# A newly searched order for the work ahead of the MLP, on five engines

## The chip, the cores and the metric

The kernel runs on one core of a Trainium2 chip. The core has five engines with an instruction queue each: TensorE (PE: matrix products and transposes, out of PSUM only by other engines), VectorE (DVE), ScalarE (ACT), GpSimd (POOL), and SyncE (SP), which here only issues DMAs; ScalarE issues some too. The metric is the time of one execution on the device in microseconds, as the median of several runs, together with one profiled execution of the kernel.

## The reference

Two layers follow each other on x of 2048 rows by 576. The first is a linear attention with 32 heads of 18 features; its feature map is a pair of softmaxes. The second is an MLP of width 4608 behind two layer norms.

```python
def _A_ref(x, wqkv, w_phi, wo):
    q, k, v = ...                                  # x @ wqkv, 32 heads of 18
    pq = jnp.einsum("bhsd,hdf->bhsf", q, w_phi)
    pk = jnp.einsum("bhsd,hdf->bhsf", k, w_phi)
    phi_q = jnp.concatenate([_softmax(pq, axis=-1), _softmax(-pq, axis=-1)], axis=-1)
    phi_k = jnp.concatenate([_softmax(pk, axis=-1), _softmax(-pk, axis=-1)], axis=-1)
    kv = jnp.einsum("bhsf,bhsd->bhfd", phi_k, v)
    z  = jnp.einsum("bhsf->bhf", phi_k)
    num = jnp.einsum("bhqf,bhfd->bhqd", phi_q, kv)
    den = jnp.einsum("bhqf,bhf->bhq", phi_q, z)[..., None] + 1e-6
    o = num / den
    return ... @ wo

def _B_ref(x, w1, b1, w2, b2):
    y = _layernorm(x, axis=-1)
    h = _gelu(jnp.einsum("bsd,df->bsf", y, w1) + b1)
    return jnp.einsum("bsf,fd->bsd", h, w2) + b2

h = x + _A_ref(_layernorm(x, axis=-1), A_wqkv, A_w_phi, A_wo)
h2 = h + _B_ref(_layernorm(h, axis=-1), B_w1, B_b1, B_w2, B_b2)
```

## The kernel before

The rows of x are taken as 16 tiles of 128, in eight pairs p = 0 to 7; a tile of a pair is called a = 0 or 1. Each layer norm is statistics on VectorE (`stats`), a power -1/2 on POOL (`power`, `power1`), and a scaling of the tile on VectorE or ScalarE (`scale`; for ScalarE POOL first works out the shift in `centre`).

The work ahead of the MLP is cut into some 60 kinds of steps, each a small function. Those that matter here:

- `load_wk`, `load_x`, `load_values`, `turn_wq`: the first loads, all issued by SyncE but one. `turn_wq` loads the query part of the weights turned, by transposing DMAs. `load_wk(c)` brings block c of the key part plainly (block 4 in two halves, called 4 and 5); TensorE turns it (`flip_mm`, line 423) into PSUM and `flip_ev` (line 429) copies it out.
- `fold_mm` (line 447) multiplies the turned weights by the block-diagonal feature weights that POOL spreads out in `spread`; `fold_ev` (line 458) casts the product from PSUM to SBUF. After it a projection of x gives the arguments of the softmaxes at once.
- `turn_n_mm` and `turn_n_ev` (line 412) turn the tiles of pairs 0 and 1 on TensorE; from pair 2 on SyncE does it by a transposing DMA (`turn_dma`, line 362).
- `key_n_mm`, `value_n_mm`, `query_n_mm` and their `_tail` (line 511) are the projections of pairs 0 and 1; `key_mm`, `value_mm`, `query_mm` (line 485) those of pairs 2 to 7, in two halves i of 18 matmuls. ScalarE takes the exponentials out of PSUM (`key_n_exp`, `key_exp`, `query_exp`, lines 575 and 548) or casts the values (`value_n_ev`, `value_ev`).
- `key_sum` and `key_n_sum` (lines 610 and 632, with a reciprocal) add up the exponentials of the keys on VectorE, and `key_weigh`, `key_n_weigh` (lines 616 and 641) scale them by it, on POOL or, where the step says `vec`, on VectorE. Each (p, i, a) is one weighing of 128 by 576.
- `sums(p, a)` (line 728) adds keys times values of a tile into `acc_kv`, after its weighings. After all sixteen, `table`, `combine_mm`, `divide`, `turn_o_mm`, `residual_mm` and `second` finish the first pair, `rescale` and `turn2_mm` make its input to the MLP, and the MLP starts (line 1326). Eight query halves are kept back to fill TensorE between these.
- `load_w1(q, n)` brings piece n of six of a quarter q of w1. Quarter 0 lies in the place of the key and query weights, quarter 1 in that of the values and keys. The MLP's first pass over w1 reads quarter 0 first.
- `warm` and `filler` are matmuls on an identity whose results nobody reads.

Three PSUM tiles of two banks (`two0` to `two2`), five tiles of exponentials (`exk`) and eleven larger tiles (`home`) are handed out by queues in the code: a step that takes a slot waits until its earlier user's result has been read.

What sets the order: the calls stand in a list in the source, and each engine executes its instructions in the order of the calls, under a manual schedule. Semaphores make each instruction wait for its data, so an engine stands when the next instruction in its row isn't ready, also if a later one would be. DMAs of SyncE and ScalarE share eight semaphores in turn, so a DMA is issued only after the one eight places ahead of it has landed. The MLP's part stands behind the list and isn't touched.

Of the kernel before, what the change touches and what calls it, by code (L numbers as in the profile page):

```python
# [47 lines left out]
def kernel(  # L48
# [889 lines left out]

    warm(6)
    filler(4)  # L940
    stats(0, 0)
    load_wk(2, syn)
    filler(4)
    filler(4)
    window_masks()
# [3 lines left out]
    filler(4)  # L949
    load_wk(0, syn)  # L950
    flip_mm(0)
    spread(2)
    power1(0, 0, pool)
    stats(0, 1)
    spread(3)
    power1(0, 1, pool)
    flip_ev(0, act)
    scale(0, 0, vec)
    turn_n_mm(0, 0)
    turn_n_ev(0, 0, act)  # L960
    load_x(2, 4, syn)
    stats(1, 0)
    spread(0)
    scale(0, 1, vec)
    load_wk(3, syn)
    load_wk(1, syn)
    flip_mm(3)
    flip_ev(3, dve)
    stats(1, 1)
    spread(1)  # L970
    filler(4)
    flip_mm(1)
    load_x(4, 6, syn)
    stats(2, 0)
    load_wk(4, syn)
    spread(4)
    flip_ev(1, act)
    power(1, pool)
    centre(1, 0)
    fold_mm("k", 2)  # L980
    fold_ev("k", 2, act)
    turn_n_mm(0, 1)
    turn_n_ev(0, 1, act)
    load_wk(5, syn)
    fold_mm("k", 1)
    fold_ev("k", 1, act)
    fold_mm("k", 0)
    flip_mm(4)
    flip_ev(4, dve)
    fold_ev("k", 0, act)  # L990
    fold_mm("k", 3)
    load_values(2, syn)
    fold_mm("k", 4)
    fold_ev("k", 3, act)
    key_n_mm(0, 0)
    stats(2, 1)
    scale(1, 1, vec)
    load_x(8, 12, syn)
    stats(4, 0)
    stats(4, 1)  # L1000
    fold_ev("k", 4, act)
    key_n_tail(0)
    scale(1, 0, act)
    key_n_exp(0, 0)
    filler(4)
    turn_n_mm(1, 0)
    key_n_mm(0, 1)
    stats(5, 0)
    power(2, pool)
    key_n_sum(0, 0)  # L1010
    turn_n_mm(1, 1)
    turn_n_ev(1, 0, act)
    key_n_mm(1, 0)
    turn_n_ev(1, 1, act)
    key_n_tail(1)
    key_n_exp(0, 1)
    key_n_sum(0, 1)
    stats(5, 1)
    key_n_mm(1, 1)
    key_n_exp(1, 0)  # L1020
    key_n_exp(1, 1)
    load_values(0, syn)
    value_n_mm(1, 1)
    turn_wq(0)
    turn_wq(2)
    load_values(1, syn)
    turn_wq(1)
    value_n_tail(1)
    value_n_ev(1, 1, act)
    fold_mm("q", 4)  # L1030
    load_b1()
    load_x(6, 8, syn)
    key_n_weigh(0, 0, 1, pool)
    power(4, pool)
    load_x(12, 16, syn)
    key_n_weigh(0, 1, 0, pool)
    swap_k(1)
    key_n_weigh(0, 1, 1, pool)
    stats(3, 0)
    stats(3, 1)  # L1040
    fold_ev("q", 4, act)
    fold_mm("q", 1)
    fold_ev("q", 1, act)
    value_n_mm(1, 0)
    value_n_ev(1, 0, act)
    scale(2, 1, vec)
    fold_mm("q", 0)
    fold_ev("q", 0, act)
    scale(4, 0, vec)
    centre(2, 0)  # L1050
    scale(2, 0, act)
    key_n_sum(1, 1)
    value_n_mm(0, 1)
    load_values(4, syn)
    swap_q(0)
    value_n_tail(0)
# [24 lines left out]
    key_n_sum(1, 0)
    stats(7, 0)
    key_n_weigh(1, 1, 0, pool)
    key_n_weigh(1, 0, 0, pool)
    key_n_weigh(1, 1, 1, pool)
    turn_dma(2)
    stats(6, 0)
    stats(7, 1)
    power(7, pool)
    scale(5, 0, vec)  # L1090
    stats(6, 1)
    key_n_weigh(1, 0, 1, pool)
    centre(7, 1)
    power(6, pool)
    query_n_exp(1, 1)
    query_n_exp(0, 0)
    scale(3, 0, act)
    query_n_exp(0, 1)
    query_n_sum(0, 1)
    query_weigh(0, 1, 1, pool)  # L1100
    key_mm(2, 0)
    key_exp(2, 0)
    turn_dma(4)
    key_mm(4, 0)
    scale(5, 1, vec)
    key_exp(4, 0)
    query_weigh(0, 0, 1, pool)
    key_sum(4, 0)
    key_weigh(4, 0, 1, pool)
    centre(6, 1)  # L1110
    key_mm(4, 1)
    load_values(3, syn)
    value_mm(2, 0)
    value_ev(2, 0, act)
    key_exp(4, 1)
    key_sum(4, 1)
    key_weigh(4, 1, 1, pool)
    key_weigh(4, 1, 0, pool)
    scale(7, 0, vec)
    key_sum(2, 0)  # L1120
    swap_q(2)
    turn_b1()
    key_mm(2, 1)
    key_weigh(4, 0, 0, pool)
    key_weigh(2, 0, 1, pool)
    value_mm(4, 0)
    key_weigh(2, 0, 0, pool)
    key_exp(2, 1)
    value_ev(4, 0, act)
    load_w1(0, 3, sca)  # L1130
    value_mm(4, 1)
    turn_dma(3)
    key_mm(3, 1)
    value_ev(4, 1, act)
    scale(6, 0, vec)
    key_sum(2, 1)
    key_weigh(2, 1, 1, pool)
    swap_q(1)
    key_weigh(2, 1, 0, pool)
    query_n_sum(0, 0)  # L1140
    query_weigh(0, 1, 0, pool)
    key_exp(3, 1)
    scale(6, 1, act)
    turn_dma(5)
    value_mm(2, 1)
    value_ev(2, 1, act)
    scale(7, 1, act)
    value_mm(3, 1)
    value_mm(5, 0)
    value_ev(5, 0, act)  # L1150
    load_w1(0, 0, syn)
    value_ev(3, 1, act)
    key_mm(5, 1)
    key_exp(5, 1)
    key_mm(3, 0)
    key_exp(3, 0)
    key_sum(5, 1)
    key_weigh(5, 1, 1, pool)
    key_mm(5, 0)
    key_sum(3, 0)  # L1160
    key_weigh(3, 0, 1, pool)
    key_exp(5, 0)
    key_sum(5, 0)
    key_sum(3, 1)
    key_weigh(3, 0, 0, pool)
    key_weigh(5, 1, 0, pool)
    load_w1(0, 5, sca)
    sums(1, 1)
    turn_dma(6)
    turn_dma(7)  # L1170
    sums(4, 0)
    sums(4, 1)
    sums(1, 0)
    query_mm(4, 0)
    query_exp(4, 0)
    load_wo(1, sca)
    load_wo(0, syn)
    load_w1(0, 4, syn)
    load_w1(0, 2, syn)
    value_mm(7, 1)  # L1180
    key_mm(6, 0)
    value_ev(7, 1, act)
    key_exp(6, 0)
    key_weigh(5, 0, 1, pool)
    key_weigh(3, 1, 1, vec)
    query_weigh(0, 0, 0, pool)
    key_weigh(3, 1, 0, pool)
    key_mm(7, 1)
    value_mm(5, 1)
    key_exp(7, 1)  # L1190
    key_sum(7, 1)
    value_ev(5, 1, act)
    key_mm(7, 0)
    key_exp(7, 0)
    key_mm(6, 1)
    key_exp(6, 1)
    value_mm(6, 1)
    value_mm(6, 0)
    value_ev(6, 0, act)
    value_ev(6, 1, act)  # L1200
    value_mm(7, 0)
    turn_q(0)
    value_ev(7, 0, act)
    load_w1(0, 1, sca)
    key_weigh(7, 1, 1, pool)
    key_sum(7, 0)
    key_weigh(7, 0, 0, pool)
    query_mm(6, 0)
    value_mm(3, 0)
    value_ev(3, 0, act)  # L1210
    query_exp(6, 0)
    key_sum(6, 0)
    key_sum(6, 1)
    query_mm(5, 1)
    key_weigh(7, 1, 0, vec)
    query_mm(2, 0)
    sums(3, 1)
    key_weigh(7, 0, 1, pool)
    sums(3, 0)
    key_weigh(5, 0, 0, pool)  # L1220
    sums(2, 1)
    key_weigh(6, 1, 1, vec)
    sums(5, 1)
    sums(7, 0)
    sums(7, 1)
    sums(5, 0)
    sums(2, 0)
    query_exp(5, 1)
    query_exp(2, 0)
    load_b2()  # L1230
    key_weigh(6, 0, 1, pool)
    key_weigh(6, 0, 0, pool)
    sums(6, 1)
# [254 lines left out]
```

## Time and profile before

| | us |
|---|---|
| three runs | 387.64, 387.71, 391.0 |
| median | 387.71 |
| the profiled execution: time | 387.87 |
| the profiled execution: span of the core | 386.1 |
| DMA, HBM read / written | 16.62 MB / 2.36 MB |

The profile's rows begin with the start and the length in us, then the engine, the line of the source, the operation, what it writes and reads, the shapes, and the number of merged instructions; in brackets stands how long the engine was idle before it and what ended that. PEld is the weight load of TensorE, which overlaps its matmuls. SPq and ACTq are the DMA issues of SyncE and ScalarE. A matmul's end is modelled, so busy TensorE can hide short stalls; the starts are measured.

### The profile page before, as it was taken

The page shows a single profiled execution, that of the slowest core. Times are in us where ns is not written, and L with a number is a line of the kernel's source. Part 1 is how long each engine was busy: PE and PEld are TensorE (multiplying, and loading weights), DVE is VectorE, ACT ScalarE, POOL GpSimd, SP SyncE. Part 2 cuts the span into 40 slices and gives each one's busy share as a digit, 9 for nine tenths or more (in the row PEclk, how much of TensorE's full clock was granted, in tenths as well). Part 3 has the DMA queues.
Part 4 walks back from the last instruction along what each step waited for, and adds up shares of the span by engine and source line. Part 5 has one row for each costly group of instructions (what it writes and reads, how often), then busy time and mean ns, then how long its engine had stood idle before and what let it go on. Part 6 is the DMA issues. An engine that isn't in the chain of part 4 may idle for free.

```text
span 386.1 us, 9945 instructions
## 1 busy us (share of the span) xinstructions
PE 380.0 (98%) x4353; PEld 265.4 (69%) x4354; DVE 166.5 (43%) x363; ACT 161.4 (42%) x289; POOL 114.3 (30%) x156
## 2 busy tenths in 40 slices
PE   7999999999999999999999999999999999999997
PEld 5677778789878887744467886444677754447773
DVE  6998997791379387670047330000560100000100
ACT  4999875698204730066630001666200026661000
POOL 6397995042425572054013101000131110000120
PEclk9999999999999999999999999999999999999999
DMA  7999998999536686450007534000071000000000
GB/s 199 270 168 187 203 217 139 256 332 244 139 69 111 108 98 121 86 119 4 0 2 97 78 87 63 2 3 0 2 120 36 17 17 0 2 2 0 17 31 16
DMA packets 72975, 35.35 MB, mean 92 GB/s; under 512 B 59940, under 2 KB 69860, under 8 KB 72804
## 3 DMA queue, kind: packets, MB, share of 16 engines
q1 hardware_dynamic: 70832, 31.23, 40.8%
q10 hardware_dynamic: 2100, 3.49, 3.9%
q8 instruction: 34, 0.56, 0.6%
q14 instruction: 9, 0.07, 0.1%
HBM read 16.62 MB, written 2.36 MB: 49 GB/s over the span
## 4 chain that ended last, share of the span: by engine, by line
PE 94%; ACT 2%; DMA 2%; DVE 1%; issue 0%; SPq 0%
PE acc L1371 37%; PE acc L1326 37%; PE two L485 10%; PE acc L868 4%; PE two L511 3%; PE acc_kv L728 1%; DMA w<-in_A_wqkv_dram 1%; ACT exk L575 1%; DMA xh<-in_A_x_dram 1%; PE acc L818 1%; PE pn L818 1%; PE two L868 1%; PE two L447 1%; DVE ob L832 1%; ACT home L412 0%; ACT shared L458 0%
## 5 line engine op out<-in xcount | busy, mean ns | idle before, releaser
L1348 ACT ACTIVATE home<-acc,b1col 128x512 bf16<-128x512 f32 (+1 forms) x180 | 98.2, 599 | 168.6 <-PE acc L1326 165.8
L1371 PE MATMUL acc<-w,home 128*128 128x288 bf16 (+2 forms) x1151 | 143.2, 286 | 0.1
L1326 PE MATMUL acc<-shared,w 64*128 64x512 bf16 (+2 forms) x1638 | 141.7, 331 | 0.2 <-ACT shared L384 0.2
L1371 PEld LDWEIGHTS <-home 128*128 128x128 bf16 x1152 | 109.4, 98 | 32.1 <-issue 1.8
L1326 PEld LDWEIGHTS <-w 64*128 64x128 bf16 x1638 | 80.4, 94 | 60.3 <-issue 1.4
L1375 DVE TENSOR_TENSOR ot<-acc,hb 128x288 bf16<-128x288 f32 (+2 forms) x32 | 14.4, 452 | 106.4 <-PE acc L1371 96.6
L1360 POOL TENSOR_TENSOR hb<-xh,b2bc 128x576 f32<-128x576 bf16 x16 | 20.4, 1273 | 104.5 <-DVE ot L1375 104.5
L674 POOL TENSOR_TENSOR padded<-home,rq 128x540 bf16<-128x540 bf16 x32 | 34.9, 1104 | 37.7 <-DVE rq L666 14.3
L877 DVE TENSOR_TENSOR xh<-acc,xh 128x288 bf16<-128x288 f32 x28 | 11.4, 447 | 69.9 <-PE acc L868 69.9
L292 POOL TENSOR_TENSOR rs<-va,mhalf 128x1 f32<-128x1 f32 x16 | 8.8, 550 | 108.7 <-DVE va L290 108.4
L485 PEld LDWEIGHTS <-home 64*128 64x128 bf16 x648 | 31.2, 94 | 8.3 <-issue 0.2
L616 POOL TENSOR_TENSOR exk<-exk,rk 128x576 bf16<-128x576 bf16 x20 | 23.6, 1219 | 0.9 <-DVE rk L612 0.9
L548 ACT ACTIVATE home<-two 128x576 bf16<-128x576 f32 x24 | 13.9, 657 | 7.9 <-PE two L485 4.5
L868 PEld LDWEIGHTS <-shared 64*128 64x128 bf16 x288 | 13.9, 94 | 4.3 <-issue 0.5
L296 DVE TENSOR_SCALAR shared<-xh,mv,rs 128x576 bf16<-128x576 bf16 x32 | 16.1, 566 | 0.5 <-DMA shared<-shared 0.5
L868 PE MATMUL acc<-wo,shared 64*128 64x288 bf16 x252 | 16.3, 283 | 0.0
L610 DVE TENSOR_REDUCE sk<-exk 128x64 f32<-128x1152 bf16 x12 | 15.9, 1326 | 0.7 <-ACT exk L548 0.7
L665 DVE TENSOR_REDUCE sk<-home 128x64 f32<-128x1152 bf16 x12 | 15.7, 1310 | 0.0
L831 DVE RECIPROCAL rec<-acc 128x18 f32<-128x18 f32 (+1 forms) x14 | 3.5, 248 | 26.8 <-PE acc L818 26.8
L485 PE MATMUL two<-wqp,home 64*128 64x288 bf16 x216 | 14.4, 283 | 0.0
L485 PE MATMUL two<-wv,home 64*128 64x288 bf16 x216 | 14.4, 283 | 0.0
L548 ACT ACTIVATE exk<-two 128x576 bf16<-128x576 f32 x24 | 13.8, 659 | 1.3 <-PE two L485 1.3
(97 smaller groups left out, 263.3 us busy)
## 6 DMA issues: line engine op xcount, KB each, us to landing
w<-in_B_w_dram SPq DMA_DIRECT2D x18, 432.0 KB, 8.4
w<-in_B_w_dram ACTq DMA_DIRECT2D x6, 432.0 KB, 11.0
out_dram<-ot SPq DMA_DIRECT2D x15, 144.0 KB, 2.2
xh<-in_A_x_dram SPq DMA_DIRECT2D x2, 576.0 KB
xh<-in_A_x_dram SPq DMA_DIRECT2D x3, 288.0 KB, 4.0
wo<-in_A_wo_dram SPq DMA_DIRECT2D x1, 648.0 KB, 6.5
wo<-in_A_wo_dram ACTq DMA_DIRECT2D x1, 648.0 KB, 11.0
w<-in_A_wqkv_dram SPq DMA_DIRECT2D x4, 158.0 KB, 3.1
```

The lines of the kernel that those rows point to most:

```text
L296: nc.vector.tensor_scalar(dst, src, mv[:, i, 0:1], rs[:, i : i + 1], ALU.subtract, ALU.mult)
L485: nc.tensor.matmul(dst[:, a, 0:HALF], lhs[rows, c, :], w[rows, slot, i * HALF : (i + 1) * HALF], start=(n == 0), stop=(n == KC - 1),)
L548: nc.scalar.activation(rows[:, :, i * HH : (i + 1) * HH, s, :], flight[key, p, i][:, :, 0:HALF].rearrange("p a (h f) -> p a h f", f=DH), A ...
L610: nc.vector.tensor_reduce(sk[:, :, :], part_of(dst, i), AX.X, ALU.add)
L616: eng.tensor_tensor(part, part, flight["r" + key, p, i][:, a, :].rearrange("p (h o) -> p h o", o=1).to_broadcast([P, NH, DH]), ALU.mult,)
L665: nc.vector.tensor_reduce(sk[:, :, :], part_of(phiq[p], i), AX.X, ALU.add)
L674: eng.tensor_tensor(padded[:, a, g0 * P : (g0 + 5) * P].rearrange("p (g k) -> p g k", k=P)[:, :, 0:STEP].rearrange("p g (h f) -> p g h f", ...
L868: nc.tensor.matmul(pa[a], oT[p % 2][rows, c, :], wo[rows, c, cs], start=(c == 0), stop=(c == KC - 1),)
L1326: nc.tensor.matmul(ph[half][:, lo:hi], w1[p_ // 9][rows, c, p_ % 9 * P : (p_ % 9 + 1) * P], ln2T[rows, c, base + lo : base + hi], start=(c ...
L1348: nc.scalar.activation(hidden(m), ph[half][:, 0:width], AF.Gelu_apprx_tanh, bias=b1col[:, m : m + 1], scale=1.0,)
L1360: nc.gpsimd.tensor_tensor(hb[:, :], xh[:, t, :], b2bc[:, :], ALU.add)
L1371: nc.tensor.matmul(po[:, :], hidden(m)[:, i_ * P : (i_ + 1) * P], w2[m // 18][:, m % 18, cs], start=(j == 0), stop=(j == NM - 1),)
```

## The change

The list of calls ahead of the MLP is replaced by another with the same steps. The instructions of TensorE fall by eight filler matmuls (and their weight loads). Some steps go to another engine: two casts of folded query weights go from ScalarE to VectorE; three more scalings of x go from VectorE to ScalarE, each with a shift on POOL; one weighing of keys goes from VectorE to POOL, and VectorE's three others are of other tiles; one copy of the turned attention result goes from VectorE to ScalarE. The key weights' halves 4 and 5 are loaded ahead of further rows of x, the transposed query weights ahead of the value weights, and piece 1 of quarter 0 of w1 later. The diff, cut to the places that matter here:

```diff
+    window_masks()
     warm(6)
-    filler(4)
-    stats(0, 0)
     load_wk(2, syn)
-    filler(4)
-    filler(4)
-    window_masks()
     filler(4)
     flip_mm(2)
     flip_ev(2, act)
-    filler(4)
     load_wk(0, syn)
     flip_mm(0)
...
+    turn_wq(2)
     filler(4)
...
+    turn_wq(1)
+    fold_mm("q", 1)
+    fold_mm("q", 3)
...
+    fold_ev("q", 3, dve)
+    fold_ev("q", 1, act)
+    fold_ev("q", 0, act)
...
+    load_values(0, syn)
+    value_n_mm(1, 0)
...
+    fold_ev("q", 4, dve)
...
-    load_w1(0, 1, sca)
...
-    key_weigh(6, 1, 0, vec)
     sums(6, 0)
+    table(0)
+    query_mm(2, 1)
+    combine_mm(1, 0, two)
+    query_exp(2, 1)
     load_w1(1, 0, sca)
...
+    query_mm(7, 1)
+    query_exp(7, 1)
+    load_w1(0, 1, sca)
```

Three places in rows of the built program follow, first the kernel before, then the changed one. Numbers behind a name tell uses of a buffer apart; the figure directly behind `two` is the PSUM slot.

ScalarE behind its first instruction, in the opening: L429 copies a turned weight block, L412 a turned half of x, L458 casts folded key weights.

```order
L429 COPY w1_0_108<-two1_172 128x5x128
L429 COPY w1_0_108<-two2_184 128x5x128
L412 COPY home0_63<-two0_205 128x512
L429 COPY w1_0_108<-two2_184 128x5x128
L458 CAST shared_109<-two0_256 128x576
L412 COPY home0_63<-two1_263 128x640
L458 CAST shared_109<-two2_272 128x576
```

```order
L429 COPY w1_0_108<-two1_155 128x5x128
L429 COPY w1_0_108<-two2_163 128x5x128
L412 COPY home0_63<-two0_190 128x512
L429 COPY w1_0_108<-two1_155 128x5x128
L458 CAST shared_109<-two0_224 128x576
L458 CAST shared_109<-two1_243 128x576
L458 CAST shared_109<-two2_259 128x576
```

The fourth row was the copy of block 1 (slot 2, shared with block 0) and is now that of block 3 (slot 1, shared with block 2); block 1 goes to VectorE, and the second half of x behind the five casts.

SyncE's loads from the second pair of key weight blocks on: L171 are key weights, L192 rows of x, L161 transposed query weights, L179 and L187 value weights.

```order
L171 DMA w1_0_108<-in_A_wqkv_dram 128x632 x2
L192 DMA xh_74<-in_A_x_dram 128x1152
L171 DMA w1_0_108<-in_A_wqkv_dram 64x632 x2
L187 DMA wv_110<-in_A_wqkv_dram 64x576
L192 DMA xh_74<-in_A_x_dram 128x2304
L179 DMA wv_110<-in_A_wqkv_dram 128x4x576
L161 DMA_TRANSPOSE w1_0_108<-in_A_wqkv_dram 128x576
L161 DMA_TRANSPOSE w1_0_108<-in_A_wqkv_dram 128x2x576
L179 DMA wv_110<-in_A_wqkv_dram 128x576
```

```order
L171 DMA w1_0_108<-in_A_wqkv_dram 128x632 x2
L171 DMA w1_0_108<-in_A_wqkv_dram 64x632 x2
L192 DMA xh_74<-in_A_x_dram 128x1152 x2
L192 DMA xh_74<-in_A_x_dram 128x2304
L161 DMA_TRANSPOSE w1_0_108<-in_A_wqkv_dram 128x576
L161 DMA_TRANSPOSE w1_0_108<-in_A_wqkv_dram 128x2x576 x2
L179 DMA wv_110<-in_A_wqkv_dram 128x4x576
L179 DMA wv_110<-in_A_wqkv_dram 128x576
```

The large load of value weights (128x4x576) stood ahead of the transposed loads and stands behind all three.

ScalarE's queue around the last sums: L548 are exponentials, L535 casts of values, L759 DMAs of w1 (into `w1_0` quarter 0, into `w1_1` quarter 1), L384 a copy of the turned attention result.

```order
L535 CAST vals_107<-two2_1275 128x2x16x18
L759 DMA w1_0_108<-in_B_w1_dram 64x3x1152
L535 CAST vals_107<-two1_1323 128x2x16x18
L548 ACTIVATE home7_70<-two0_1304 128x2x16x18 x2
L548 ACTIVATE home8_71<-two2_1353 128x2x16x18 x2
L548 ACTIVATE home9_72<-two1_1373 128x2x16x18 x2
L759 DMA w1_1_1518<-in_B_w1_dram 64x3x1152 x2
```

```order
L548 ACTIVATE home8_71<-two1_1512 128x2x16x18 x2
L759 DMA w1_1_1545<-in_B_w1_dram 64x3x1152
L548 ACTIVATE home10_73<-two2_1572 128x2x16x18 x2
L759 DMA w1_0_108<-in_B_w1_dram 64x3x1152
L548 ACTIVATE home9_72<-two1_1594 128x2x16x18 x2
L384 COPY shared_109<-pT_1621 128x512
L759 DMA w1_1_1545<-in_B_w1_dram 64x3x1152
```

The last piece of quarter 0 stood three exponentials ahead of the first pieces of quarter 1, and now stands behind one of them.

More of the change, by code (lines that the diff above doesn't have):

```diff
@@ L1133 @@
[L1133 to L1155, printed above, removed]
```

526 lines of the change are left out of this document (270 added, 256 removed).

## The prediction

> **What bounds the kernel now.** The busy shares come first, then a table of stages cut at four places: 5.65 us (first real transposes on TensorE), 24.39 (first sums of keys times values), 65.64 (last sums issued) and 80.06 (first MLP matmul).
>
> ```profile
> PE 380.0 (98%) x4353; PEld 265.4 (69%) x4354; DVE 166.5 (43%) x363; ACT 161.4 (42%) x289; POOL 114.3 (30%) x156
> ...
> core 0: us, PE busy (x) PEld busy (x) DVE busy (x) ACT busy (x) POOL busy (x), PEclk, DMA share, GB/s
> 5.65:24.39 18.74, 17.22 (x190) 12.67 (x189) 17.33 (x44) 16.95 (x29) 11.02 (x21) 1.00 0.97 239
> 24.39:65.64 41.25, 41.25 (x724) 32.53 (x721) 38.02 (x52) 33.51 (x58) 36.51 (x41) 1.00 1.04 189
> 65.64:80.06 14.42, 13.95 (x232) 10.94 (x230) 10.80 (x32) 8.84 (x17) 1.12 (x2) 1.00 0.92 229
> 80.06:386.10 306.04, 303.30 (x3195) 206.64 (x3195) 97.63 (x230) 100.63 (x184) 61.82 (x72) 1.00 0.32 61
> ```
>
> TensorE sets the end. A new order can give back only holes on it: none in the third stage (41.25 of 41.25), 18.74 - 17.22 = 1.52 us in the second, 14.42 - 13.95 = 0.47 in the fourth, and what short stalls the modelled ends of matmuls hide. The fifth stage, 306 us, keeps its instructions. So the gain is capped near 2 us plus what fillers cost, while a loss has no cap. The timeline shows the opening, by SyncE, TensorE and ScalarE (start, length, instructions). Behind it stand sizes with median times from issue to landing, and the shortest, median and longest landing of the six loads of key weights (L171).
>
> ```profile
> 1.24 0.89 SPq L171 DMA_DIRECT2D w<-in_A_wqkv_dram  x2
> 7.68 0.42 SPq L179 DMA_DIRECT2D wv<-in_A_wqkv_dram  x1
> 8.15 4.86 SPq L161 DMA_TRANSPOSE w<-in_A_wqkv_dram  x2
> 13.68 1.37 SPq L161 DMA_TRANSPOSE w<-in_A_wqkv_dram  x1
> ...
> 1.41 2.74 PE L285 MATMUL two<-ident 128*128 128x512 bf16 x6 [1.41 <-POOL ones L210]
> 3.94 1.91 PE L276 MATMUL acc_kv<-ident 128*128 128x128 bf16 x16
> 5.65 0.50 PE L423 MATMUL two<-ident,w 128*128 128x128 bf16 x5
> 8.16 0.45 PE L423 MATMUL two<-ident,w 128*128 128x128 bf16 x5 [0.57 <-DMA w<-in_A_wqkv_dram]
> 8.45 0.43 PE L447 MATMUL two<-w 128*128 128x126 bf16 x5
> 21.43 1.50 PE L511 MATMUL two<-wv,home 128*128 128x288 bf16 x12
> 23.14 1.15 PE L511 MATMUL two<-wv,home 128*128 128x288 bf16 x8
> 24.12 0.43 PE L447 MATMUL two<-w 128*128 128x126 bf16 x5
> ...
> 8.65 0.69 ACT L429 COPY w<-two 128x640 bf16<-128x640 bf16 x1 [0.69 <-PE two L423]
> 10.36 2.36 ACT L458 CAST shared<-two 128x576 bf16<-128x576 f32 x4
> 12.60 0.88 ACT L308 ACTIVATE shared<-xh,nb,rs 128x576 bf16<-128x576 bf16 x1
> 13.37 1.19 ACT L575 ACTIVATE exk<-two 128x576 bf16<-128x576 f32 x2
> 15.38 0.69 ACT L412 COPY home<-two 128x640 bf16<-128x640 bf16 x1 [0.34 <-PE two L407]
> 15.97 3.38 ACT L575 ACTIVATE exk<-two 128x576 bf16<-128x576 f32 x6
> ...
> wv<-in_A_wqkv_dram SPq DMA_DIRECT2D x1, 576.0 KB, 6.2
> wv<-in_A_wqkv_dram SPq DMA_DIRECT2D x1, 144.0 KB, 4.2
> home<-shared SPq DMA_TRANSPOSE x6, 3.8
> ...
> DMA to landing us min/median/max: 2.9/3.1/4.3
> ```
>
> From about 6 to 25 us ScalarE is the chain (16.95 of 18.74 busy): it empties PSUM, and TensorE waits for slots. The copy of a weight block at 8.65 (L429) came late because its transposes waited for a load until 8.16.
>
> **The change, part by part.**
>
> *Opening.* Block 2 of the key weights is issued at 1.24 and block 0 ends its issue at 2.13. With the median landing of 3.1 us block 2 is there near 4.8; block 0, third in the queue, at 5.2 to 6.4, and I take 6.1. One filler group now follows the warm-up instead of four, so TensorE stands from 4.37 (four fillers at 107 ns, from 16 of them between 3.94 and 5.65) to 4.8, and again from 5.35 to 6.1. Eight of 28 filler matmuls are gone in all. ScalarE then runs without the 0.69 us hole: block 0 copied from 6.6, the first turned half of x from 7.2, block 3 from 7.75. Casts of folded keys come 0.57 us apart ((2.36 - 0.64) / 3) at 8.3, 8.95, 9.75, 10.3 and 10.85. The third waits because block 1 still arrives at 8.16 and its copy, by VectorE, frees a slot only near 9.1. The second turned half follows at 11.4, the scaling at 12.0 (before 12.60), the first exponentials at 12.75 (before 13.37), the six others at 15.2 to 18.55 (before 15.97 to 19.35): 0.6, then 0.8 us ahead.
>
> *Folded queries and values.* Here most of that lead goes. The query folds need slots that the last exponentials hold until 18.55, so TensorE stands about 0.8 us; two more scalings of x on ScalarE (0.88 each) stand among the evictions, against two casts given to VectorE. From 19.15 TensorE runs without a hole: four value halves of 0.98 (23.14 to 24.12), two tails of 0.35 (1.50 with a tail, 1.15 without) and one fold of about 0.3, to 24.1. The same work ended at 24.39 before: 0.3 gained. But the large load of value weights is moved behind the three transposed loads. Those take SyncE 4.86 + 1.37 = 6.2 us from about 7.6, so it is issued near 14.4 instead of 7.68 and lands 4.2 to 6.2 later, 18.6 to 20.6, where 19.15 is needed. The nearer row is the large one, but it was queued behind much more; I take 19.35, 0.2 lost. Turned halves of x have less room in the third stage: SyncE's transposes of pairs 4 and 6 follow ScalarE's scalings near 26.5 and 42.4, take 3.8, and are needed at about 31.0 and 46.7. That is 0.7 and 0.5 spare, cost 0. Opening and values together: -0.1, with ends at -1.5 (the second stage's holes gone) and +1.2.
>
> *Weighings.* POOL and VectorE scale the keys in time for the last sums. The rows are POOL's first weighing, VectorE's sums, and the weighings of both engines with shortest, median and longest duration.
>
> ```profile
> 17.54 1.16 POOL L641 TENSOR_TENSOR exk<-exk,rk 128x576 bf16<-128x576 bf16 x1 [3.94 <-DVE rk L637]
> ...
> L610 DVE TENSOR_REDUCE sk<-exk x12: 1294/1342/1353, 34.0 to 58.6; 128x64 f32<-128x1152 bf16 x12
> ...
> L616 POOL TENSOR_TENSOR exk<-exk,rk x20: 1159/1168/1686, 36.2 to 61.5; 128x576 bf16<-128x576 bf16 x20
> ...
> L616 DVE TENSOR_TENSOR exk<-exk,rk x4: 744/1244/1716, 52.0 to 63.8; 128x576 bf16<-128x576 bf16 x4
> ...
> 60.50 4.01 DVE L616 TENSOR_TENSOR exk<-exk,rk 128x576 bf16<-128x576 bf16 x3
> 65.75 0.50 DVE L743 TENSOR_TENSOR kvm<-acc_kv,wmask 128x324 bf16<-128x324 f32 x1 [1.24 <-PE acc_kv L728]
> ```
>
> VectorE keeps three weighings of four, POOL gets one more (28 + 1 = 29) and starts at 20.5 instead of 17.54, since the first sum of keys waits for the last exponentials and takes 1.34 and a reciprocal of some 0.5. With 29 x 1.17 = 33.9, and 8 us of other work (the third stage's 36.51 less 24 weighings leaves 8.4), it ends at 62.4; I find one wait of 2.0 for a sum that four statistics stand ahead of on VectorE: 64.4. The last sums need it at 65.1, so 0.7 is spare: cost 0. If every one of VectorE's three runs into POOL's at the 1716 of its slowest instead of 744, it is 2.9 more, and 2.2 late; that is the upper end. Nothing is gained below, since TensorE has no hole there.
>
> The DVE rows show weighings that take 744 alone and (4.01 / 3) 1337 ns beside POOL's. [...]
>
> *Table, division, residual.* The sequence of two covering query blocks between combine and turn is kept, and so is the wait on VectorE's division; one of two copies after it goes to ScalarE, hidden beside the query block behind it. Cost 0, at most +-0.47 (the fourth stage's hole).
>
> *First MLP weights.* One of the six pieces of the first quarter of w1 was issued by ScalarE at 58.09. It now stands behind an exponential of the query, after the first piece of the next quarter.
>
> ```profile
> 58.09 0.62 ACTq L759 DMA_DIRECT2D w<-in_B_w_dram  x1
> 65.87 1.54 ACTq L759 DMA_DIRECT2D w<-in_B_w_dram  x2
> ...
> w<-in_B_w_dram SPq DMA_DIRECT2D x18, 432.0 KB, 8.4
> w<-in_B_w_dram ACTq DMA_DIRECT2D x6, 432.0 KB, 11.0
> ...
> DMA to landing us min/median/max: 4.8/8.6/13.5
> ...
> 80.06 4.18 PE L1326 MATMUL acc<-shared,w 64*128 64x128 bf16 x85 [0.17 <-ACT shared L384]
> ```
>
> Two query blocks and two combines after 65.64 put its issue near 68.9, and the second matmul of the MLP reads it at 79.95. Landing may take 11.05. The rows say 8.6 (all), 11.0 (ScalarE's queue), 13.5 (the slowest): 0 to 2.5 us late. It is second in its queue behind one piece, where the slowest case is presumably the third of three, so I take 10.5: on time, cost 0. SyncE's weights move only among themselves; the rest of MLP weights is needed 10 us later or more.
>
> *Sum.* -0.1 + 0 + 0 + 0 = -0.1 on the profiled 387.87: 387.8. The median of the runs shown, 387.71, stands 0.16 below that execution, so I forecast 387.6. Own range of this case: 386.4 to 388.3.
>
> **Rivals.**
>
> *MLP weights late* (slower): the moved piece of w1 takes 12.1 instead of 10.5, between 11.0 and 13.5, or ScalarE's next load, which waits for an older one, holds back the copy that feeds the MLP. It decides from 11.05 on. For it: the median of that queue is within 0.1 of the limit. Against: only one piece lies ahead of it. Price 1.05: 388.7.
>
> *A late clock* (slower): TensorE issued 128-column matmuls every 107 ns until 5.65, and 5 in 0.29 us at 8.16 (58 ns each). It had then worked since 1.41 without a hole. The new holes at 4.37 and 5.35 may postpone this. [...] No run here yet shows whether a gap of 0.4 counts.
>
> *Values late* (slower): the load lands at 20.6. TensorE has no other work in order there: 1.2 lost, 388.8.
>
> *Weighings late* (slower): POOL ends 1.2 late through overlap with VectorE: 388.8. For it: both engines are busy 36 to 38 of 41 us in that stage. Against: VectorE has three scalings fewer.
>
> *The loads land as before and all holes go* (faster): 1.4 gained, 386.2. Against it: ScalarE's chain stays, and it gains 0.8 at most.
>
> **How the numbers follow.** Forecast 0.42; MLP weights late 0.26; late clock 0.12; values late 0.08; weighings late 0.09; all holes gone 0.03. Nearly all of it lies between 386.4 and 389.4, the slow cases with 0.5 on top; two of them together, or one beyond its bound, are left out with the 386.2. A change of 1% is 3.9 us, about what a measurement of this kernel can tell from none. Faster by that would need more than all holes: 0.02. Slower by that needs three mishaps or a wait not found here: 0.05. Within 1%: 0.93.
>
> **What would show it.** Right: block 3 copied by ScalarE near 7.75, six exponentials ending near 18.6, values done near 24.1, the last sums issued near 65.5, MLP from 79.9 with no DMA named ahead of it. Wrong: 107 ns matmuls after 6.1; a DMA as releaser of the first MLP weights or of value matmuls; TensorE waiting for POOL or VectorE between 60 and 66; a hole in the third stage, where now there is none.

## The result, and the profile after

| | before | after |
|---|---|---|
| median of six runs each | 387.86 us | 393.17 us |
| lowest and highest | 387.64, 391.0 | 392.53, 394.64 |
| ratio, with its 95% interval | | 1.0134 (1.011 to 1.0158) |
| the profiled execution: time, span | 387.87, 386.1 | 394.64, 392.9 |

The changed kernel is slower by 1.3%, where no change was forecast, and the time lies outside the range (386.4 to 388.3). The profiled execution of it is its slowest, 1.5 us above the median. Its stages follow with the same columns. The first border stays at 5.65 us, the others are at the same events as before (values done, last sums issued, first MLP matmul):

```profile
5.65:24.05 18.40, 16.65 (x178) 12.17 (x179) 17.45 (x44) 17.39 (x30) 11.46 (x26) 1.00 1.02 233
24.05:68.10 44.05, 41.83 (x722) 33.44 (x720) 42.31 (x50) 34.31 (x60) 37.16 (x41) 1.00 0.89 170
68.10:82.55 14.45, 14.04 (x233) 10.66 (x230) 10.33 (x30) 8.56 (x15) 1.11 (x2) 1.00 0.95 202
82.55:392.90 310.35, 305.07 (x3198) 207.82 (x3196) 97.76 (x230) 101.57 (x185) 61.87 (x72) 0.99 0.32 63
```

The stages changed by -0.34, +2.80, +0.03 and +4.31 us. The third stage has a hole now (44.05 of span, 41.83 busy). The MLP lost 4.3 us: it stood for 310.35 - 305.07 = 5.28 instead of 2.74, and its same matmuls took 1.77 us more at a granted clock of 0.99.

*Around the last sums*, in the timeline of the changed kernel:

```profile
54.51 7.89 POOL L616 TENSOR_TENSOR exk<-exk,rk 128x576 bf16<-128x576 bf16 x7
...
55.93 7.76 DVE L616 TENSOR_TENSOR exk<-exk,rk 128x576 bf16<-128x576 bf16 x2
...
62.29 3.03 PE L728 MATMUL acc_kv<-vals,exk 128*128 128x57 bf16 x93
...
63.61 1.34 DVE L610 TENSOR_REDUCE sk<-exk 128x64 f32<-128x1152 bf16 x1
65.05 0.55 DVE L612 RECIPROCAL rk<-sk 128x64 f32<-128x64 f32 x1
65.68 1.16 POOL L616 TENSOR_TENSOR exk<-exk,rk 128x576 bf16<-128x576 bf16 x1 [3.28 <-DVE rk L612]
65.71 1.75 DVE L616 TENSOR_TENSOR exk<-exk,rk 128x576 bf16<-128x576 bf16 x1
67.52 0.65 PE L728 MATMUL acc_kv<-vals,exk 128*128 128x57 bf16 x17 [2.20 <-DVE exk L616]
```

VectorE's two weighings of pair 7 took 7.76 us. The first of them took 7.09 and ended 0.62 after POOL's row of weighings (54.51 + 7.89 = 62.40), the second took 0.75. These two are new on VectorE; (6, 1, 1) it had before, too, and (3, 1, 1), its weighing at 52 in the kernel before, is POOL's now. Behind the two stands the last sum of keys on VectorE; POOL waits 3.28 for that, and TensorE 2.20 for the weighing behind it. The same view of the kernel before has one row of sums:

```profile
62.39 3.32 PE L728 MATMUL acc_kv<-vals,exk 128*128 128x57 bf16 x110
```

So the sums begin 0.10 earlier (62.29) and take 68.10 - 62.29 = 5.81 instead of 3.25: +2.56.

*At the MLP's start*, in the same timeline of the changed kernel:

```profile
82.55 0.23 PE L1327 MATMUL acc<-shared,w 64*128 64x128 bf16 x1
...
83.30 0.45 PE L1327 MATMUL acc<-shared,w 64*128 64x128 bf16 x9 [0.53 <-DMA w<-in_B_w_dram]
...
84.48 0.60 ACTq L759 DMA_DIRECT2D w<-in_B_w_dram  x1
...
85.18 0.59 ACT L384 COPY shared<-two 128x512 bf16<-128x512 bf16 x1 [3.54 <-DMA w<-in_B_w_dram]
...
85.82 19.27 PE L1327 MATMUL acc<-shared,w 64*128 64x128 bf16 x332 [2.06 <-ACT shared L384]
```

TensorE waits twice: 0.53 for the moved piece of w1 (0, 1), and 2.06 for a copy by ScalarE. That copy had its input since 82; in ScalarE's queue the load of piece (1, 2) stood ahead of it, and this load could not be issued before an older one on its semaphore had landed. The chain of waits shows that:

```profile
70.12 14.34 DMA w<-in_B_w_dram
84.46 0.02 issue
84.48 0.60 ACTq L759
```

Behind these holes the clock falls. The windows (the column third from the right) have it at half for 3.4 us (0.71, 0.50 and 0.93 of three stretches of 2 us); a stretch of 2 us holds 22 matmuls instead of some 42:

```profile
84.00:86.00 2.00, 0.18 (x7) 0.18 (x8) 1.97 (x3) 0.82 (x2) 0.55 (x1) 1.00 1.08 269
86.00:88.00 2.00, 2.00 (x44) 1.84 (x40) 1.97 (x3) 1.98 (x3) 2.00 (x4) 0.71 1.08 315
88.00:90.00 2.00, 2.00 (x22) 1.73 (x20) 1.97 (x3) 1.83 (x6) 2.00 (x3) 0.50 1.10 331
90.00:92.00 2.00, 2.00 (x38) 1.95 (x36) 0.69 (x2) 1.49 (x4) 0.27 (x2) 0.93 1.06 244
```

The whole account of the profiled pair: up to the sums -0.10, their wait +2.56, division +0.03, the two waits of the MLP +2.59, its matmuls at half clock +1.77: 6.85, where the spans differ by 6.8.

### The profile page after: what moved, and what is told of

The parts are those of the page before. It is cut to its first block, busy times and chain, and to the rows that moved or that the text cites. A ratio compares the mean times of both kernels' runs of the same rounds, so it can differ in the third digit from the quotient of the medians.

```text
span 392.9 us, 9935 instructions
## 1 busy us (share of the span) xinstructions
PE 381.8 (97%) x4346; PEld 266.3 (68%) x4346; DVE 170.6 (43%) x360; ACT 163.8 (42%) x291; POOL 115.1 (29%) x160
## 4 chain that ended last, share of the span: by engine, by line
PE 79%; DVE 13%; DMA 4%; ACT 1%; issue 1%; SPq 0%; POOL 0%; ACTq 0%; DVEq 0%
PE acc L1327 36%; PE acc L1372 36%; PE acc L868 4%; DVE sk L610 4%; DMA w<-in_B_w_dram 4%; DVE exk L616 2%; DVE rk L612 2%; DVE sk L632 1%; DVE st L330 1%; PE two L511 1%; DVE sk L656 1%; DVE shared L355 1%; PE acc L818 1%; DVE rk L637 1%; PE pn L818 1%
## 5 line engine op out<-in xcount | busy, mean ns | idle before, releaser
L1349 ACT ACTIVATE home<-acc,b1col 128x512 bf16<-128x512 f32 (+1 forms) x180 | 98.5, 599 | 169.3 <-PE acc L1327 166.4
L1327 PE MATMUL acc<-shared,w 64*128 64x512 bf16 (+2 forms) x1638 | 143.4, 334 | 2.6 <-ACT shared L384 2.1
L1327 PEld LDWEIGHTS <-w 64*128 64x128 bf16 x1638 | 81.5, 95 | 63.3 <-issue 3.2
L1376 DVE TENSOR_TENSOR ot<-acc,hb 128x288 bf16<-128x288 f32 (+2 forms) x32 | 14.3, 451 | 106.1 <-PE acc L1372 96.3
L548 ACT ACTIVATE home<-two 128x576 bf16<-128x576 f32 x24 | 14.1, 650 | 10.1 <-PE two L485 10.1
L485 PE MATMUL two<-shared,home 64*128 64x288 bf16 x216 | 14.2, 283 | 0.0
```

The costliest lines, as they stand in the source:

```text
L485: nc.tensor.matmul(dst[:, a, 0:HALF], lhs[rows, c, :], w[rows, slot, i * HALF : (i + 1) * HALF], start=(n == 0), stop=(n == KC - 1),)
L1327: nc.tensor.matmul(ph[half][:, lo:hi], w1[p_ // 9][rows, c, p_ % 9 * P : (p_ % 9 + 1) * P], ln2T[rows, c, base + lo : base + hi], start=(c ...
L1349: nc.scalar.activation(hidden(m), ph[half][:, 0:width], AF.Gelu_apprx_tanh, bias=b1col[:, m : m + 1], scale=1.0,)
L1376: nc.vector.tensor_tensor(ot[:, cs], po[:, :], hb[:, cs], ALU.add)
```

## The experiments

Three causes were to be told apart: the places of VectorE's weighings, the places of the loads, and lateness that passes from one to the other. The runs came in groups on several chips, with medians of the kernel before of 387.64 to 388.64; each is compared with that of its own group. The four kernels called rows (turns, turns_late, turns_pair, turns_long) compute nothing of the reference.

**The held copy: one load behind it.**

```diff
-    load_w1(1, 2, sca)
...
     turn2_ev(0, 1, act)
     query_exp(3, 0)
+    load_w1(1, 2, sca)
```

> The changed kernel, with one load moved: ScalarE's piece 2 of quarter 1 of w1 stands behind the copy that feeds the MLP, not ahead of it. Theory (the load, which waits for an older load on its semaphore, holds the copy back): the 2.06 us that the third group of MLP matmuls waits for ScalarE's copy go, the 0.53 us wait for piece 1 of quarter 0 stays: 393.2 - 2.1 = 391.1 us. Rival (weights as such come too late, since all of them are issued 2.5 us later than before): the MLP waits for a DMA instead, 392.5 to 393.2 us.

Measured: 393.19 (392.64 to 396.32), ratio 1.0115 (1.0084 to 1.0147), which is within the interval of the changed kernel. The time is the rival's, and TensorE waits longer than before for the moved piece of w1 (1.15). The timeline of the profiled execution, the slowest of the six, shows where the rest went:

```profile
82.36 0.59 ACT L384 COPY shared<-two 128x512 bf16<-128x512 bf16 x1 [0.51 <-PE two L379]
...
84.14 3.14 PE L1327 MATMUL acc<-shared,w 64*128 64x128 bf16 x71 [1.15 <-DMA w<-in_B_w_dram]
87.71 0.60 ACTq L759 DMA_DIRECT2D w<-in_B_w_dram  x1
...
90.26 16.50 PE L1327 MATMUL acc<-shared,w 64*128 64x256 bf16 x270 [2.98 <-ACT home L1349]
```

The copy is no longer held, but now the load holds ScalarE's first gelus (L1349), and TensorE waits 2.98 for them. The held copy is explained as expected, and the repair is not one: what waits in this queue holds whatever stands behind it.

**The same load from SyncE's queue.**

```diff
-    load_w1(1, 2, sca)
+    load_w1(1, 2, syn)
```

> The changed kernel with piece 2 of quarter 1 of w1 issued by SyncE at the same place of the order, so that ScalarE's queue holds no load ahead of the MLP's copy nor of its first gelus. Theory (ScalarE stands in the load's wait for an older one): the copy follows its transposes, 2.06 us of the MLP's wait go, and a wait of 0.5 to 1.2 us for piece 1 of quarter 0 stays: 393.2 - 2.1 = 391.1 us; where the clock then keeps its full rate, 1.5 less, 389.6. Rival (weights as such come late): the MLP waits for them as long, 392.5 us or more.

Measured: 393.71 (391.64 to 396.83, four runs), ratio 1.0169 (1.0107 to 1.023). In its profile ScalarE holds nothing up, and only a wait of 1.07 for the moved piece is left, as expected:

```profile
83.84 0.58 ACT L384 COPY shared<-two 128x512 bf16<-128x512 bf16 x1 [0.51 <-PE two L379]
...
85.53 9.69 PE L1327 MATMUL acc<-shared,w 64*128 64x128 bf16 x191 [1.07 <-DMA w<-in_B_w_dram]
```

The time did not follow. The runs differ by their clock: 391.64 at 1.0, 392.98 and 394.44 at 0.996, 396.83 at 0.991. In the profiled one (392.98) the half clock came, as far as its rows tell, behind the sums' wait of 2.2: VectorE waited 1.3 there for the first product of the division, 0.57 in the changed kernel, and the MLP's 191 matmuls in the row above went at 51 ns each.

**Both pieces moved.**

```diff
     load_w1(0, 3, sca)
+    load_w1(0, 1, sca)
...
     query_exp(7, 1)
-    load_w1(0, 1, sca)
...
-    load_w1(1, 2, sca)
...
     query_exp(3, 0)
+    load_w1(1, 2, sca)
```

> As the kernel with the late piece, and piece 1 of quarter 0 of w1 goes back ahead of the last sums (behind piece 3 on ScalarE). Theory (two separate waits at the MLP's start, 2.06 and 0.53 us): 393.2 - 2.6 = 390.6 us, the MLP goes on without a wait named for a DMA. Rival (the early load takes DMA time from others, or holds ScalarE up at its new place): no better than the kernel with the late piece, about 391.1 us.

Measured: 392.16 (391.96 to 392.25). The MLP starts at 84.18 without a wait, as the theory has it. The loss against the kernel before falls from 5.3 to 3.8 us only (392.16 less 388.33), where 2.3 was expected. In the profiled execution the clock fell behind the wait of the sums (2.19 us; 2.20 in the changed kernel, where it had not fallen there):

```profile
66.00:68.00 2.00, 0.20 (x5) 0.20 (x6) 1.75 (x1) 0.00 (x0) 1.13 (x1) 0.86 0.14 30
68.00:70.00 2.00, 2.00 (x29) 1.50 (x28) 1.06 (x4) 0.00 (x0) 0.00 (x0) 0.50 0.02 4
```

That is not the whole reason: two of the four runs had a mean clock of 1.0 and took 391.96 and 392.25 all the same. What they lost in its place is not shown.

**All loads at the old places.** In the changed kernel:

```diff
     value_ev(7, 1, act)
+    load_w1(0, 1, sca)
...
+    load_b2()
     sums(6, 1)
     sums(6, 0)
+    load_w1(1, 0, sca)
+    load_w1(1, 1, syn)
+    load_w1(1, 2, sca)
+    load_w1(1, 3, syn)
+    load_w1(1, 5, syn)
     table(0)
     query_mm(2, 1)
     combine_mm(1, 0, two)
     query_exp(2, 1)
-    load_w1(1, 0, sca)
+    load_w1(1, 4, sca)
+    load_w2(0, 0, syn)
...
```

> The changed kernel with the loads of the MLP's weights (and of b2) at the places of the kernel before; the rest of its order stays, the late weighings too. Theory (the waits at the MLP's start, 2.6 us in the profile, and the clock at half speed behind them, about 1.7 us, come from where these loads stand): only the wait of the last sums stays, 388.3 + 2.5 - 0.1 = 390.7 us, up to 391.5 if that wait alone also halves the clock, as in the profile of the kernel with both pieces moved. Rival (the weights come late because the sums end late, wherever the loads stand): 392.5 us or more.

Measured: 392.05 (390.56 to 392.2, eight runs), ratio 1.0067 (1.0047 to 1.0088). The runs fall into two heaps: three at 390.56 to 390.65 with a mean clock of 1.0, five at 392.03 to 392.2 with 0.996. The profile is of the first kind. Its MLP starts at 82.55, as in the changed kernel, with no wait, and its span ends at 388.8: 306.25 us for the MLP instead of 310.35.

```profile
82.55 12.71 PE L1327 MATMUL acc<-shared,w 64*128 64x128 bf16 x237
```

So all 4.1 us that the MLP lost in the profile come from where the loads stand. The heaps price the half clock: 1.5 us, in one and the same program.

**The new loads in the kernel before.** The same moves backwards.

> The kernel before, with the loads of the MLP's weights (and of b2) at the places that they have in the changed kernel. Theory: the waits at the MLP's start come with them, 388.3 + 2.6 = 390.9 us, and up to 392.6 where the clock halves behind them. Rival (they only hurt behind late sums): 388.8 us or less.

Measured: 390.93 (389.72 to 393.42, ten runs), ratio 1.0054 (1.0032 to 1.0075). The loads hurt with sums in time, too. In the profiled execution, the longest of these runs, ScalarE stands for 3.99 ahead of the copy, and TensorE 3.65 behind it, with the clock at half for 6.8 us:

```profile
82.00 0.60 ACTq L759 DMA_DIRECT2D w<-in_B_w_dram  x1
82.69 0.59 ACT L384 COPY shared<-two 128x512 bf16<-128x512 bf16 x1 [3.99 <-DMA w<-in_B_w_dram]
...
83.33 11.89 PE L1326 MATMUL acc<-shared,w 64*128 64x128 bf16 x184 [3.65 <-ACT shared L384]
```

**VectorE's last sum ahead of its weighings.** From here on the weighings, in the changed kernel:

```diff
+    key_sum(6, 1)
     key_weigh(7, 0, 1, vec)
     key_weigh(7, 0, 0, vec)
...
-    key_sum(6, 1)
```

> The changed kernel, with VectorE's last sum of keys ahead of its two weighings of pair 7. Theory S (a weighing on VectorE gets no turn while POOL's weighings follow each other without a gap): POOL runs through to 63.5, VectorE's three weighings end at 64.1, 64.8 and 65.5, the sums end near 66.8 instead of 68.1: 391.9 us. Rival T (VectorE gets a turn after one POOL weighing, as in the kernel before): three weighings of 1.7 from 57.8, no wait left: 390.7 us. Rival O (these weighings are slow by their own operands, 7.1 + 0.75 + 1.75): the last ends at 67.4, no gain: 393 us.

Of three weighings in a row, the first was 6.51 us long and ended 0.6 behind POOL's row (52.23 + 11.28 = 63.51); all were done at 65.45, and the sums ended at 66.83:

```profile
52.23 11.28 POOL L616 TENSOR_TENSOR exk<-exk,rk 128x576 bf16<-128x576 bf16 x10
57.60 7.85 DVE L616 TENSOR_TENSOR exk<-exk,rk 128x576 bf16<-128x576 bf16 x3
```

These are the numbers of theory S for this row, and T and O fall. But the time, 393.89 (393.03 to 395.0), did not fall by the 1.3: the MLP waited 0.77 for a load and 2.02 for the held copy, and the mean clock was 0.991 to 0.996. The gain was given back there.

**POOL made to stand.**

```diff
     key_weigh(7, 0, 0, vec)
+    key_sum(6, 1)
+    key_weigh(6, 1, 0, pool)
     key_weigh(6, 0, 1, pool)
...
-    key_sum(6, 1)
...
-    key_weigh(6, 1, 0, pool)
```

> The changed kernel, with POOL's weighing of (6, 1, 0), which needs VectorE's last sum, moved ahead of five of its other weighings, so that POOL stands at about 56.8 us. Theory S and rival T (the duration is a wait for POOL): VectorE's first weighing ends within 0.7 us of POOL's stand, 1.5 us long instead of 7.1, and POOL goes on near 60.0 and ends near 66.8; sums end near 68, time 393 +- 0.7. Rival O (slow by its operands): it stays near 7.1, POOL waits until 65 and ends near 70.6: 397 us.

VectorE's first weighing took 1.47 instead of 7.09, ending 0.61 after the last one that POOL did before it stood:

```profile
52.49 4.53 POOL L616 TENSOR_TENSOR exk<-exk,rk 128x576 bf16<-128x576 bf16 x4
...
56.16 2.14 DVE L616 TENSOR_TENSOR exk<-exk,rk 128x576 bf16<-128x576 bf16 x2
```

That excludes O. The sums ended at 68.97, not near 68, and the time was 395.25 instead of 393: POOL stood for 3.37 and was then held once by VectorE's third weighing, which came first (0.76 long, POOL's 1.71).

**What in the row decides?** Six kernels, VectorE's weighing always one of 128 by 576. The core of the first, of which the next two vary the delay, and the number and the readers of VectorE's weighings:

```python
def trial(k, wait, told):
    nc.vector.reciprocal(rk[:, k, :], rk[:, k, :])
    for n in range(N):
        weigh(nc.gpsimd, chain[k][:, n, :], rk[:, k, :])
        if told:
            nc.scalar.copy(seen[:, k * N + n, :], chain[k][:, n, 0:4])
    for w in wait:
        nc.vector.reciprocal(late[:, 0:w], late[:, 0:w])
    weigh(nc.vector, mine[:, :], rk[:, k, :])
```

> A kernel of its own that computes nothing of the reference: 18 times POOL does six weighings of 128x576 one behind the other, and VectorE comes in the midst of them with one weighing of another tile, after a delay by reciprocals of 0 to 128 elements. In the first nine nobody reads POOL's results until the end of the six, in the last nine ScalarE reads a few elements of each, so that each signals its end. [...] Theory S2 (it always waits for the end of the row): 4 to 7 us in all. Theory S3 (what decides is when it comes within a POOL weighing): short and long ones in both halves, by the delay. Rival T (turns): 0.7 to 1.9 us in all.

> As the kernel with eighteen trials, but POOL does nine weighings in a row, and VectorE's comes later: 0.3 us into the first of them, or about one to five weighings later. Six trials without a signal from each of POOL's, six with one. Theory D (the longer POOL's instructions have followed each other, the less they leave a gap; a wait or a signal closes the row up): late arrivals without signals wait to the end of the nine (up to 10 us), early ones for one (1.6 us), and those with signals for one. Rival T (turns at any time): 0.7 to 1.9 us in all twelve; what made VectorE's weighing wait for six of POOL's is then not shown by such a row alone.

> Rows of eight POOL weighings as before, with VectorE's coming 1.4 to 4.8 us into the row. In trials 1, 2, 11 and 12 VectorE has one weighing; in trials 3 to 6, 9 and 10 two in a row, the first without a signal of its own (its consumer waits for the second); in trials 7 and 8 two, each with a signal. Theory G (a VectorE weighing that signals nothing, with another behind it, is not served until POOL's row ends, as in the changed kernel; one that signals is served after one POOL weighing): the first of the two is 3 to 8 us long in trials 3 to 6, 9 and 10, and at most 1.7 in the others. Rival T (the signal does not matter): at most 1.9 us in all twelve.

Here are, from the view of that line in each of the three, VectorE's weighings with shortest, median and longest duration:

```profile
L95 DVE TENSOR_TENSOR mine<-mine,rk x18: 693/1227/1627, 68.0 to 201.9; 128x576 bf16<-128x576 bf16 x18
```

```profile
L95 DVE TENSOR_TENSOR mine<-mine,rk x12: 1187/1357/1528, 68.0 to 196.8; 128x576 bf16<-128x576 bf16 x12
```

```profile
L95 DVE TENSOR_TENSOR mine<-mine,rk x20: 1325/1462/1714, 75.8 to 192.9; 128x576 bf16<-128x576 bf16 x20
```

In all 50 VectorE got its turn after one POOL weighing at most (693 to 1714 ns), whether POOL's weighings signalled each its end or not: rival T in all three. S2, S3 and G fall, and D as far as these rows go. The same in the kernel, where an exchange of the two weighings gives each its signal:

```diff
-    key_weigh(7, 0, 1, vec)
     key_weigh(7, 0, 0, vec)
+    key_weigh(7, 0, 1, vec)
```

> The changed kernel with one exchange: VectorE's two weighings of pair 7 change places, so that TensorE's sums wait for each by itself and each gets a signal; nothing else moves. Theory G (the first of them stood because it signals nothing): they take about 1.7 us each, end near 59.3 instead of 63.7, VectorE's last weighing ends near 63, the wait of the last sums (2.4 us) goes: sums end at 65.6 to 65.9, 393.2 - 2.4 = 390.8 us. Rival (they wait for the end of POOL's row whatever they signal): the first stays near 7 us, 393.2 us.

It stayed at 7.05 us, and 393.49. In the three rows' kernels POOL had gone on for about 6 us at most when VectorE came (an estimate: 0.3 and five weighings of 1.16 us). In the changed kernel POOL works without a gap from 33.28 to 62.40, as its windows show, and VectorE came at 55.93:

```profile
33.28:62.40 29.12, 29.12 (x489) 23.20 (x486) 28.47 (x27) 24.25 (x43) 29.12 (x31) 1.00 1.00 190
```

In the kernel before, POOL had worked without a gap since 38.46 when VectorE's three weighings came at 60.50, about as long, but VectorE had had a turn at 52:

```profile
38.46 7.89 POOL L616 TENSOR_TENSOR exk<-exk,rk 128x576 bf16<-128x576 bf16 x7 [0.86 <-DVE rk L612]
...
51.99 0.78 DVE L616 TENSOR_TENSOR exk<-exk,rk 128x576 bf16<-128x576 bf16 x1
```

That such a turn is enough is argued from this profile and not tried alone. The last two runs try the length: one has longer rows, the other a gap at this place.

> A kernel of its own that computes nothing of the reference. Four rows of 30 POOL weighings without a gap, VectorE's weighing 6, 12 and 22 us into the row, and in the fourth 15 us into it behind sums and reciprocals instead of reciprocals; then a row of eight, with a VectorE weighing that waits for a matmul in the same instruction. Theory L (what decides is how long POOL has gone on without a gap: 22 us in the changed kernel, 6 in the kernel before, at most 6 in the rows tried so far): one POOL weighing at 6 us, the rest of the row (12 us and more) at 12 to 22 us. Theory M (VectorE's wait for TensorE in the same instruction): long in the fifth alone. Rival T: at most 1.9 us in all five; the cause stays open.

VectorE's five weighings, from the timeline of that kernel (POOL's rows start at 85.00, 119.69, 154.38, 189.06 and 223.75):

```profile
91.18 1.19 DVE L95 TENSOR_TENSOR mine<-mine,rk 128x576 bf16<-128x576 bf16 x1
...
133.00 0.78 DVE L95 TENSOR_TENSOR mine<-mine,rk 128x576 bf16<-128x576 bf16 x1
...
178.38 10.26 DVE L95 TENSOR_TENSOR mine<-mine,rk 128x576 bf16<-128x576 bf16 x1
...
204.51 0.88 DVE L95 TENSOR_TENSOR mine<-mine,rk 128x576 bf16<-128x576 bf16 x1
...
226.38 1.39 DVE L95 TENSOR_TENSOR mine<-mine,rk 128x576 bf16<-128x576 bf16 x1
```

At 6, 13 and 15 us into a row it waited for one weighing at most; at 24 us it stood for 10.26, to the end of the row (154.38 + 33.64 = 188.02). L holds with a bound later than I had put it, M and T fall. In that third row VectorE's own reciprocals ahead were the longest, too (24.25 us). The next run leaves VectorE's work ahead of its weighings as it is in the changed kernel and breaks only POOL's row:

```diff
     key_weigh(7, 1, 0, pool)
-    key_weigh(3, 0, 0, pool)
+    key_weigh(7, 0, 0, pool)
     key_weigh(7, 0, 1, vec)
-    key_weigh(7, 0, 0, vec)
+    key_weigh(3, 0, 0, vec)
```

> The changed kernel with two weighings exchanged between the engines: POOL takes (7, 0, 0), which needs a sum that VectorE ends at 55.9, and VectorE takes (3, 0, 0). Each does as many as before, but POOL stands for about 0.3 us just ahead of VectorE's first weighing. Theory L (a gap in POOL's row lets VectorE in, and after it one POOL weighing at a time): VectorE's two weighings take at most 1.7 us each, its last sum ends near 61, the wait of the last sums goes: 393.2 - 2.4 = 390.8 us. Rival (in this place VectorE waits for the end of the row whatever is ahead): one or both stay 6 to 7 us long: 393.2 us.

```profile
56.08 2.39 DVE L616 TENSOR_TENSOR exk<-exk,rk 128x576 bf16<-128x576 bf16 x2
56.12 9.52 POOL L616 TENSOR_TENSOR exk<-exk,rk 128x576 bf16<-128x576 bf16 x7 [0.32 <-DVE rk L612]
60.50 0.76 DVE L616 TENSOR_TENSOR exk<-exk,rk 128x576 bf16<-128x576 bf16 x1
```

A gap of 0.32 us is enough. VectorE's first weighing started in it, the second waited for one of POOL's (2.39 for both), the third took 0.76, and the sums were done at 65.97 instead of 68.10. The time is 392.0 (390.7 to 393.19), ratio 1.0096 (1.0073 to 1.0119): the loss against the kernel before falls from 5.3 to 3.4 us, about what the sums gained. What is left in the profile, the fastest of the four runs, is at the MLP's start, which waits 1.93 for a load; the other three had a mean clock of 0.995 to 0.996.

**Both repaired.** The old loads, VectorE's sum first, and the sums in another order, of which the calls of `sums` are shown:

```diff
     sums(3, 1)
     sums(5, 1)
     sums(2, 1)
     sums(5, 0)
-    sums(7, 0)
     sums(3, 0)
-    sums(7, 1)
     sums(2, 0)
-    sums(6, 1)
     sums(6, 0)
+    sums(7, 1)
+    sums(7, 0)
+    sums(6, 1)
```

> The changed kernel with the loads at the old places, VectorE's last sum of keys ahead of its weighings, and the last sums of keys times values in the order in which their weighings then end: the four that need VectorE's (of tiles 7 and 6) come last. Theory (late weighings and loads are all of the loss): POOL ends at 63.5, VectorE at 65.5, sums end at 65.9 instead of 65.64 before, no wait at the MLP's start: 388.3 + 0.2 = 388.5 us, as before. Rival (something else in the new order costs too): above 389.5 us.

Measured: 388.36 (388.23 to 389.7, ten runs) against 388.51 of the kernel before on the same chip: ratio 0.9987 (0.9967 to 1.0008), all runs at clock 1.0. The sums end at 65.84, the MLP starts at 80.50 without a wait:

```profile
62.34 3.58 PE L728 MATMUL acc_kv<-vals,exk 128*128 128x57 bf16 x110
...
80.50 14.76 PE L1327 MATMUL acc<-shared,w 64*128 64x128 bf16 x274
```

So these two places hold the whole loss, as far as the interval tells, and the rest of the new order, its opening too, is worth nothing that can be measured. No run points to a version that beats both.

## Why the prediction was wrong, step by step

A loss of 1% or more had a chance of 0.05, for three mishaps "or a wait not found here". There were two such waits, and the clock behind them.

*Opening and values: right in time*, and with them the third stage up to 62. ScalarE's rows are near the forecast times (7.75 for block 3, 18.55 for the end of the exponentials; 14.99 + 3.38 = 18.37):

```profile
7.56 0.69 ACT L429 COPY w<-two 128x640 bf16<-128x640 bf16 x1
...
14.99 3.38 ACT L575 ACTIVATE exk<-two 128x576 bf16<-128x576 f32 x6
```

Values were done at 24.05 (24.1), and the sums began 0.10 earlier, the forecast size. The way there was partly another: TensorE turned blocks 2 and 0 of the key weights from 4.37 on without the two forecast holes, and stood 0.80 ahead of 6.40 for VectorE's scaling of x instead. That the totals agree is in part luck. Fillers of 128 columns came every 55 ns from 6.64 on ((7.08 - 6.64) / 8), so "a late clock" fell as it was put (in the opening), and "values late" too. No run shows a price of the late clock, which the forecast's 389.4 for the slow cases took in.

*Weighings: wrong, +2.56 instead of 0.* The term failed in "If every one of VectorE's three runs into POOL's at the 1716 of its slowest". That bound came from four weighings of a kernel in which VectorE came in 8 us after its last turn; here one took 7091 ns. I had also asked only when POOL ends. Its row did end early (62.40, but for one weighing; forecast 64.4 with it); the late engine was VectorE, with the last sum queued behind its weighings, and POOL's last weighing waited for that sum and ended at 66.84. The rival "weighings late" had the place, but the wrong engine, and half the price. The 2.2 that I called the upper end are near the measured 2.56 by chance, and the range of the sum left them out. VectorE's sums did not pay beside POOL: ten of its twelve took 1294 to 1297 ns, the first 1344, and the one where POOL stood 1339. In the short rows its weighings waited for one of POOL's at most (1714 ns the longest), in the long ones for six to nine (7091 and 10255 ns).

*Table, division, residual: right*, +0.03.

*First MLP weights: wrong, +2.59 instead of 0, and +1.77 behind it.* The moved piece was mis-sized: issued at 71.37, 2.5 later than forecast since the sums were late, it took 11.9 instead of 10.5, 0.53 late (its rival said 1.05). What failed as a step is "the rest of MLP weights is needed 10 us later or more": TensorE waited for none of the others in the profile, but ScalarE's piece (1, 2), in the kernel before the second of its two loads at 65.87, had come to stand in its queue ahead of the copy that feeds the MLP, and a load waits there for an older load to land, 14.34 us after that was issued. The rival named this in half a sentence and gave it no price of its own.

*The clock behind a hole was not in the sum at all.* It was weighed only for the opening. In the changed kernel it went to 0.50 for 3.4 us behind the two holes at the MLP (2.59 together) and not behind the 2.20 at the sums, where in both_pieces 2.19 was enough. One program meets it in some executions and not in others (after_old_loads: a mean clock of 1.0 in three runs, 0.996 in five).

## What to carry to other kernels

An instruction that waits for another engine's, as VectorE's weighings did for POOL's (at most 1.7 us in short rows, 7.09 and 10.26 in long ones), is to be priced by the other's row in which it comes, not by the slowest that a profile happens to have; a gap of 0.3 us in a long row may be worth microseconds. When a DMA is moved in the queue of an engine that also computes, look first at which older DMA it waits for, and at what stands behind it. A hole of some 2 us on TensorE can have a second price, 1.5 us of half clock in one program here, and a repair of one wait shows in the time only if the next is repaired, too.

## What was not expected of the hardware

- VectorE's weighing waited for all that was left of POOL's row after 22 to 24 us of POOL's work without a gap and without a turn of VectorE's (six weighings in the changed kernel, nine in a bare row), but for one at most up to 15 us. The four timelines of the new order that show this row unbroken have it, at 6.5 to 7.1 us (7.09 in the changed kernel, 7.05 in weigh_swapped, 6.5 in sum_first and all_cured). That the length decides is shown by one bare row and one gap; that a turn of VectorE's ends it, by the kernel before alone; what in the length does it, stays open.
- The clock fell to 0.50 for 3.4 us, in one profile (before_new_loads) for 6.8. In the changed kernel its changes lie whole multiples of 3.41 us apart (full from 4.93, half from 86.85, full from 90.26: 24 and 1). In the six profiles whose windows show a fall, TensorE had stood for 1.8 to 2.5 us of the 3.41 just ahead of it (worked out from these windows and the timelines: 1.84 in both_pieces, 2.06 in the changed kernel, 2.20 in sum_first, 2.32 in before_new_loads, 2.48 in late_piece, 2.51 in pool_pause). In the changed kernel the hole of 2.20 at the sums brought none. Counted on from 4.93 in steps of 3.41, an estimate from the three changes, a border lies within it at 66.37, with 1.07 us ahead and 1.15 behind. What decides is not shown: no run tried it. One program has the fall in some executions and not in others, 1.5 us apart in one; in two others (both_pieces, weigh_swapped) the runs with a mean clock of 1.0 are not set apart from those with 0.996.
- Of the MLP's loads of 432 KB, issued one behind the other after the sums, the one that TensorE waited for took 11.9 us to land and the one that held ScalarE's queue 14.3, where the median of w1's pieces was 8.6 in the kernel before and the slowest 13.5.
